# Attention with an MLP on one core: the probability products of two half cycles issued in one block at the end of a cycle

## The chip, the core and the metric

The kernel runs on one core of a Trainium2 chip. The core has five engines that run side by side: TensorE (PE in the profile; its weight loads are PEld) multiplies matrices into PSUM, VectorE (DVE) and ScalarE (ACT) read PSUM and compute elementwise, GpSimd (POOL) works on SBUF only, and SyncE (SP) starts most of the DMA transfers. Each takes its own instructions in order, and semaphores hold one until another engine is done. The metric is the time of one execution in microseconds of the device, less being better.

## The reference: what is computed

One transformer layer on 2048 rows of 512 numbers, with 32 query heads of 16 and one shared key and value head, adaptive layer norms around attention and MLP (`mod` comes from a condition vector).

```python
h = _layernorm(x) * (1 + ca) + sa
q = (h @ wq) -> 32 heads of 16;  k = h @ wk;  v = h @ wv
p = softmax(q k^T * 16 ** -0.5)          # 32 heads x 2048 queries x 2048 keys
x = x + ga * ((p @ v) @ wo)
h = _layernorm(x) * (1 + cb) + sb
x = x + gb * (gelu(h @ w1 + b1) @ w2 + b2)   # 512 -> 1376 -> 512
```

## The kernel before

**Tiles and units.** The queries are cut into 8 blocks of 256 rows and the heads into 8 groups of 4; one pair of the two is a unit, 64 units in all, in order (line 456). A unit goes through the 2048 keys in 8 steps of two 128-key tiles (line 1322). Two steps, X = K and Y = K + 1, make a cycle of the main loop (line 1366), so a unit has four cycles, K = 0, 2, 4, 6, and the loop 256.

**What a step does.** `sexp` (line 584) multiplies a key tile with the queries of two heads, 64 rows of the array by 512 columns, and ScalarE takes the exponential of the product (tile e) into a probability tile p: four such products and exponentials a step, for j = 0, 1 and for s = 0, 1, where s names the upper or lower 64 rows of the array, which work at the same time. The product lands in one PSUM bank of three, e0, e1 or e2, which the caller names; each bank has one buffer (line 591), so the next product in a bank waits until ScalarE has read the one before. `pv` (line 600) multiplies the p tile of a step with the values: 16 products of 128 rows by 32 columns of the array and 256 columns of p, four of them side by side in four column groups, added up over the unit in one PSUM tile (acc, bank v). The p tiles have three buffers (line 590). `end_step` (line 1356) calls `pv` and, after the last step of a unit, `finish_unit`, which has ScalarE copy acc out of PSUM.

**Maxima ahead.** The softmax takes off the row maximum, which is found ahead of time. `Max.step` (line 507) multiplies the queries of a later unit with 512 keys (tile m, three PSUM banks) and VectorE reduces the product to its maximum (line 522). About 8 such steps go into each cycle, four in each half.

**Fill.** The other matrix products (the query projection qps, the output product wops, transposes tp, the MLP's w1ps and w2ps) are cut into batches, and `take` (line 1191) hands one batch to a cycle. Each product of a batch is done in two halves of 64 rows (`half`, line 189): the upper halves in half X of the cycle, the lower ones in half Y, beside the exponent and score products that use the other rows. What follows a batch (bias, GELU, splitting a number into a high and a low part) is put off by `later` and run by `due` at a count of the `clock`, which advances four times a cycle.

**The order of a cycle** (lines 1400 to 1445) is written out by hand, and each engine executes in that order. Half X issues score products, exponent products and the upper halves of the batch; then the products of the step before (`behind`, that is Y of the cycle before); then half Y; then the products of X; Y is left behind for the next cycle. Which bank each exponent product uses is written into three variants:

- heavy, a batch of more than 4.8 (in products of 512 columns; lines 1417 to 1420 and 1433 to 1438): the order of banks is e0, e1, e2, e0 in half X and e0, e1, e2, e0 in half Y, the last of each on the rows of the fill;
- light, a smaller batch (`light_half`, line 1404): each half begins and ends its own rows with e0, and uses e1 and e2 on the other rows;
- without a batch (`plain`, line 1386): e1, e2, e0, e1 in half X and e2, e0, e1, e2 in half Y.

Before the main loop lies a stretch of some 90 us that loads, normalises and projects; after it a tail finishes the last block.

Of the kernel before, what the change touches and what calls it, by code (L numbers as in the profile page):

```python
# [52 lines left out]
def adaln_mqa_mlp(  # L53
# [99 lines left out]
    def due():  # L153
        now = [p for p in pending if p[0] <= clock[0]]
        pending[:] = [p for p in pending if p[0] > clock[0]]
        for _, fn in now:
            fn()
# [31 lines left out]
    def half(one, s):  # L189

        ps, a, b_, first_, last_ = one
        rows = slice(64 * s, 64 * s + 64)
        nc.tensor.matmul(ps, a[rows], b_[rows], start=first_ and s == 0, stop=last_ and s == 1)  # L193
# [390 lines left out]
    def sexp(u, K, j, s, bank):  # L584

        w = blocks[units[u][0]][1]
        qst = qsts[u]
        assert u in placed
        if (u, K) not in ptiles:
            ptiles[u, K] = att.tile([P, 2, 2, 512], F32, name=f"p{u}_{K}", tag="p", bufs=3)  # L590
        e = psum.tile([P, 512], F32, name=f"e{u}_{K}_{j}_{s}", tag="x" if bank == "x" else f"e{bank}", bufs=1)
        rows = slice(64 * s, 64 * s + 64)
        if w == 512:
            kt, rhs = K, qst[rows, j, :]
        else:
            kt, rhs = 2 * K + j, qst[rows].rearrange("p j n -> p (j n)")
        nc.tensor.matmul(e, ks[rows, kt * P:(kt + 1) * P], rhs, start=True, stop=True)  # L597
        nc.scalar.activation(ptiles[u, K][:, j, s, :], e, AF.Exp, scale=0.25)  # L598

    def pv(u, K):  # L600
        w = blocks[units[u][0]][1]
        if K == 0:
            accs[u] = psum.tile([P, w], F32, name=f"acc{u}", tag="v")
        pt = ptiles.pop((u, K))
        for kt in ([K] if w == 512 else [2 * K, 2 * K + 1]):
            for cidx in range(4):
                s, j = divmod(cidx, 2)
                rhs = pt[:, j, s, :] if w == 512 else pt[:, kt - 2 * K, s, j * w:(j + 1) * w]
                ins = nc.tensor.matmul(accs[u][32 * cidx:32 * cidx + 32, :], va[:, kt, :], rhs,  # L609
                                       start=kt == 0, stop=kt == NKT - 1)  # L610
                if kt % 2 or cidx:
                    wait_early(ins)
# [563 lines left out]
    def resume():  # L1176

        go_on(holder[0])

    def advance():  # L1180

        for job in holder or list(queue):
            while not held and job[0] <= clock[0] and go_on(job):
                pass
            if held or holder:
                break

    def put_off(*jobs):
        queue.extend([0, job, False] for job in jobs)

    def take():
        advance()
        return held.pop() if held else None
# [133 lines left out]
    def products(batch):  # L1327

        return sum(b_.shape[-1] * (4 if b_.dtype == F32 else 1) for _, _, b_, _, _ in batch) / 512
# [6 lines left out]
    def issue(*groups):  # L1336

        at = [0.0] * len(groups)
        groups = [list(g) for g in groups]
        while any(groups):  # L1340
            g = min((g for g in range(len(groups)) if groups[g]), key=lambda g: at[g])
            length, fn = groups[g].pop(0)
            fn()
            at[g] += length

    def mixture(a, b):

        out = []
        while a or b:
            if a:  # L1350
                out.append(a.pop(0))
            if b:
                out.append(b.pop(0))
        return out

    def end_step(u, K):

        pv(u, K)
        if K == steps[u] - 1:
            finish_unit(u)  # L1360
            if units[u][1] == NQ - 1:
                put_off(rest(units[u][0], units[u][0] == len(blocks) - 1))

    behind = None
    for u in range(NU):
        for K in range(0, steps[u], 2):
            goal = lead[u] + (lead[u + 1] - lead[u]) * (K + 2) / steps[u]
            goal = min(goal, first[u + QBUFS] if u + QBUFS < NU else first[NU])
            n = max(0, 2 * round((goal - mp.done) / 2))

            def maxes(s, n, first_=1.0, held=None):
                return [(1.0 if i else first_, lambda i=i: mp.step(s, held if i == 2 else None)) if mp.has(s) else (0.0, lambda: None)
                        for i in range(n)]

            def exps(s, which):
                return [(1.0, lambda K=K, j=j, bank=bank: sexp(u, K, j, s, bank)) for K, j, bank in which]

            def halves(batch, s):

                total = products(batch)  # L1380
                if total <= LIGHT:
                    return [(products([one]), lambda one=one: half(one, s)) for one in batch]
                ahead = AHEAD if total > BATCH - 0.5 else (BATCH - (1.5 if batch[-1][4] else 0.5)) / total
                return [(ahead * products([one]), lambda one=one: half(one, s)) for one in batch]

            def plain(s, K, t, n, banks):

                a, b_, c_, d = banks
                ms, other = maxes(s, n), maxes(t, n)

                if not holder and mp.has(s) and n > 1:
                    ms[0] = 1.0, lambda: mp.step(s, tag="x", bufs=1)
                one = mixture(exps(s, [(K, 0, a), (K, 1, c_)]), ms)
                issue(one, exps(t, [(K, 0, b_)]) + other + exps(t, [(K, 1, d)]))

            X, Y = K, K + 1

            due()  # L1400
            batch = take() if behind else None
            light = batch and products(batch) <= LIGHT

            def light_half(s, K):

                mine, fill = exps(s, [(K, 0, 0), (K, 1, 0)]), halves(batch, s) + ([(0.0, go_on_)] if s else [])
                ms, es = maxes(1 - s, n // 2), exps(1 - s, [(K, 0, 1), (K, 1, 2)])
                issue(mine[:1] + fill + mine[1:], ms[:1] + es[:1] + ms[1:3] + es[1:] + ms[3:])

            def go_on_():  # L1410
                resume()
                for fn in reduces or ():
                    fn()

            if light:
                light_half(0, X)
            elif batch:
                groups = [mixture(maxes(1, n // 2, 0.0), exps(1, [(X, 0, 0), (X, 1, 1), (Y, 0, 2)])),
                          halves(batch, 0) + exps(0, [(X, 0, 0)])]
                issue(*(reversed(groups) if batch[0][3] else groups))  # L1420
            else:
                plain(1, X, 0, (n + 2) // 4, (1, 2, 0, 1))
            clock[0] += 1
            due()
            if behind:
                end_step(*behind)
            clock[0] += 1
            due()
            if light:
                reduces = None  # L1430
                light_half(1, Y)
                advance()
            elif batch:

                reduces = [] if batch[-1][4] else None
                issue(mixture(maxes(0, n // 2, 0.0, reduces), exps(0, [(X, 1, 0), (Y, 0, 1), (Y, 1, 2)])),
                      halves(batch, 1) + [(0.0, go_on_)] + exps(1, [(Y, 1, 0)]))
                advance()
            else:
                plain(1, Y, 0, n // 4, (2, 0, 1, 2))  # L1440
            clock[0] += 1
            due()
            end_step(u, X)
            behind = (u, Y)
            clock[0] += 1
            if state["mods"] and "w2" not in preps:
                preps["w2"] = prep_w2()
            if clock[0] >= prepared[0] + PREP and weights and weights[0] in preps:
                prepared[0] = clock[0]
                if next(preps[weights[0]], 0) == 0:  # L1450
                    weights.pop(0)
# [51 lines left out]
```

## Time and profile before

| | |
|---|---|
| median of 3 runs | 1586.05 us (1585.31 to 1586.48) |
| profiled execution | 1589.15 us, its span 1587.3 us |
| TensorE busy in the span | 1562.7 us (98%) |
| VectorE busy | 1406.0 us (89%) |
| ScalarE busy | 1204.3 us (76%) |
| GpSimd busy | 692.8 us (44%) |
| mean granted TensorE clock | 0.992 |

A group's row gives the line, the engine, the operation, output and inputs by the program's names, the count, the busy time and the mean of one, and the idle time ahead of it. In the timeline a row gives the start within the span, the length, and how many equal instructions in a row are merged in it (x16); cuts of the timeline merge differently. A wait "A x <- B y: total, times, longest" says that engine A sat idle ahead of x until B had done y. The ends of matmuls are modelled; their starts are records. In the 1465 us from 80 to 1545 us, in which the main loop lies, the granted TensorE clock was 1.00.

### The profile page before, as it was taken

The numbers are of one execution on the slowest core, as the hardware profiler recorded it, in microseconds if no ns is written. First come the engines' busy times: TensorE is split into PE (matmuls) and PEld (weight loads), VectorE is DVE, ScalarE is ACT, GpSimd is POOL, SyncE is SP. The second block draws the span as 40 slices with busy tenths as digits, with TensorE's granted clock in tenths as the row PEclk, the third lists the DMA queues.
The fourth block names the chain that finished last, engine by engine and source line by source line (L and its number), as shares of the span: only waits on it lengthen the run. The fifth ranks groups of instructions, "written<-read, shape, count | busy, mean of one in ns | idle before, by whom it ended". The sixth has DMA issues, their size and how long they took to land.

```text
span 1587.3 us, 43409 instructions
## 1 busy us (share of the span) xinstructions
PE 1562.7 (98%) x17491; PEld 1043.9 (66%) x17491; DVE 1406.0 (89%) x2491; ACT 1204.3 (76%) x2417; POOL 692.8 (44%) x1242
## 2 busy tenths in 40 slices
PE   5999999999999999999999999999999999999999
PEld 3556655567766676666766676666766677676667
DVE  6889999899999998999999999999999999999715
ACT  5477777778877887778877887778877788778853
POOL 4345447446513472345622464334712465324721
PEclk8899999999999999999999999999999999999999
DMA  7135423312012120212112130212112130121231
GB/s 263 67 108 177 141 70 101 100 33 97 32 56 67 56 86 23 90 35 94 46 40 86 44 99 19 70 54 86 56 32 92 35 108 22 60 72 50 94 139 68
DMA packets 81022, 121.74 MB, mean 77 GB/s; under 512 B 15966, under 2 KB 55646, under 8 KB 80564
## 3 DMA queue, kind: packets, MB, share of 16 engines
q1 hardware_dynamic: 80804, 118.95, 22.6%
q8 instruction: 137, 2.24, 0.6%
q14 instruction: 65, 0.53, 0.1%
q10 hardware_dynamic: 16, 0.00, 0.0%
HBM read 91.13 MB, written 27.27 MB: 75 GB/s over the span
## 4 chain that ended last, share of the span: by engine, by line
PE 94%; ACT 3%; DVE 1%; DMA 1%; issue 0%; SPq 0%; POOL 0%; DVEq 0%; ACTq 0%
PE acc L609 32%; PE e L597 19%; PE m L517 19%; PE w1ps L193 8%; PE w2ps L193 6%; PE wops L193 3%; PE qps L193 2%; ACT p L598 2%; PE w2ps L187 2%; PE w1ps L187 1%; DVE mx L522 1%; PE tp L193 1%; PE kps L164 1%; PE tp L371 0%; PE modr L289 0%; DMA wm<-in_w_mod_dram 0%
## 5 line engine op out<-in xcount | busy, mean ns | idle before, releaser
L522 DVE TENSOR_REDUCE mx<-m 128x1 f32<-128x512 f32 x2048 | 1271.6, 681 | 105.6 <-PE m L517 95.6
L598 ACT ACTIVATE p<-e 128x512 f32<-128x512 f32 x2048 | 1066.6, 601 | 290.5 <-PE e L597 198.9
L517 PE MATMUL m<-ks,qst 64*128 64x512 f32 x2048 | 829.4, 433 | 6.4 <-DVE ve L205 4.9
L597 PE MATMUL e<-qst,ks 64*128 64x512 f32 x2048 | 729.5, 411 | 2.0 <-ACT wqH L334 1.3
L609 PE MATMUL acc<-p,va 128*32 128x256 f32 x8192 | 550.2, 385 | 1.7 <-DMA qst<-dq 1.7
L517 PEld LDWEIGHTS m<-ks,qst 64*128 64x128 f32 x2048 | 367.4, 184 | 104.6 <-DVE mx L522 85.7
L597 PEld LDWEIGHTS e<-qst,ks 64*128 64x128 f32 x2048 | 356.9, 184 | 112.6 <-ACT p L598 102.6
L609 PEld LDWEIGHTS acc<-p,va 128*32 128x32 f32 x8192 | 214.6, 109 | 219.6 <-issue 113.3
L193 PE MATMUL w1ps<-h2H,w1t 64*128 64x256 f32 x1232 | 236.6, 288 | 0.0
L193 PEld LDWEIGHTS w1ps<-h2H,w1t 64*128 64x128 f32 x1232 | 184.0, 185 | 31.7 <-issue 22.2
L566 POOL TENSOR_SCALAR mt<-turned 8x32 f32<-8x32 f32 x256 | 53.5, 209 | 342.7 <-DVE turned L572 330.6
L193 PE MATMUL w1ps<-h2L,w1t 64*128 64x256 f32 x616 | 169.5, 275 | 0.0
L193 PE MATMUL w2ps<-w2H,gH 64*128 64x256 f32 (+1 forms) x546 | 161.0, 295 | 0.0
L193 PE MATMUL w2ps<-w2H,gL 64*128 64x256 f32 (+1 forms) x546 | 153.9, 282 | 0.0
L193 PE MATMUL w2ps<-w2L,gH 64*128 64x256 f32 (+1 forms) x546 | 153.4, 281 | 0.0
L193 PEld LDWEIGHTS w1ps<-h2L,w1t 64*128 64x128 f32 x616 | 113.7, 185 | 0.0
L193 PEld LDWEIGHTS w2ps<-w2H,gH 64*128 64x128 f32 x546 | 100.5, 184 | 11.7 <-issue 5.4
L193 PEld LDWEIGHTS w2ps<-w2H,gL 64*128 64x128 f32 x546 | 100.7, 184 | 1.7
L193 PEld LDWEIGHTS w2ps<-w2L,gH 64*128 64x128 f32 x546 | 100.7, 184 | 1.3
L949 POOL TENSOR_SCALAR tt<-tt 128x256 f32<-128x256 f32 x77 | 31.2, 406 | 143.8 <-ACT tt L948 143.8
L193 PE MATMUL wops<-woH,onH 64*128 64x256 f32 x224 | 67.9, 303 | 0.0
L193 PE MATMUL wops<-woL,onH 64*128 64x256 f32 x224 | 62.2, 278 | 0.0
(220 smaller groups left out, 1613.1 us busy)
## 6 DMA issues: line engine op xcount, KB each, us to landing
w1t<-dw SPq DMA_DIRECT2D x82, 512.0 KB
qst<-dq SPq DMA_DIRECT2D x128, 64.0 KB
do<-oc SPq DMA_DIRECT2D x64, 128.0 KB
dw<-w1s SPq DMA_DIRECT2D x11, 512.0 KB
xt<-in_A_x_dram SPq DMA_DIRECT2D x4, 1024.0 KB
dq<-qH SPq DMA_DIRECT2D x16, 256.0 KB
dq<-qL SPq DMA_DIRECT2D x16, 256.0 KB
qst<-dq SPq DMA_DIRECT2D x128, 32.0 KB
```

What stands on the lines that cost most here:

```text
L164: nc.tensor.matmul(ps, a, b_, start=begin and n == 0, stop=end and n == last)
L187: nc.tensor.matmul(ps, a, b_, start=first_, stop=last_)
L193: nc.tensor.matmul(ps, a[rows], b_[rows], start=first_ and s == 0, stop=last_ and s == 1)
L517: nc.tensor.matmul(m, qsts[u][rows, j, t * P:(t + 1) * P], ks[rows, kc * 512:(kc + 1) * 512], start=True, stop=True)
L522: nc.vector.tensor_reduce(out=self.mx[u][:, i, kc:kc + 1], in_=m, axis=AX.X, op=ALU.max)
L566: nc.gpsimd.tensor_scalar(out=mt[:, g:g + 32], in0=turned[g:g + 4 * T, :], scalar1=1.0, scalar2=0.0, op0=ALU.mult, op1=ALU.add)
L597: nc.tensor.matmul(e, ks[rows, kt * P:(kt + 1) * P], rhs, start=True, stop=True)
L598: nc.scalar.activation(ptiles[u, K][:, j, s, :], e, AF.Exp, scale=0.25)
L609: ins = nc.tensor.matmul(accs[u][32 * cidx:32 * cidx + 32, :], va[:, kt, :], rhs, start=kt == 0, stop=kt == NKT - 1)
L949: nc.gpsimd.tensor_scalar(out=tt, in0=tt, scalar1=1.0, scalar2=1.0, op0=ALU.mult, op1=ALU.add)
```

## The change

The products of the step before are issued in the middle of the cycle only in the first cycle of a unit (K = 0), where they are the last ones of the unit before and its sums are then copied out. In the other three cycles they are issued at the end of the cycle, directly ahead of the products of X: 32 products in one block where there were two blocks of 16 with half Y between them. The first line only keeps the condition for taking a batch as it was, as `behind` may now be empty. Banks, buffers, batches and the counts of the clock are untouched.

```diff
@@ -1398,7 +1398,7 @@
             due()
-            batch = take() if behind else None
+            batch = take() if u or K else None
             light = batch and products(batch) <= LIGHT
@@ -1422,8 +1422,9 @@
                 plain(1, X, 0, (n + 2) // 4, (1, 2, 0, 1))
             clock[0] += 1
             due()
-            if behind:
+            if behind and K == 0:
                 end_step(*behind)
+                behind = None
             clock[0] += 1
             due()
             if light:
@@ -1440,6 +1441,8 @@
                 plain(1, Y, 0, n // 4, (2, 0, 1, 2))
             clock[0] += 1
             due()
+            if behind:
+                end_step(*behind)
             end_step(u, X)
             behind = (u, Y)
             clock[0] += 1
```

## The prediction

> **What bounds the kernel now.** I read the page first, for the shares and the chain of waits.
>
> ```profile
> PE 1562.7 (98%) x17491; PEld 1043.9 (66%) x17491; DVE 1406.0 (89%) x2491; ACT 1204.3 (76%) x2417; POOL 692.8 (44%) x1242
> ...
> PE 94%; ACT 3%; DVE 1%; DMA 1%; issue 0%; SPq 0%; POOL 0%; DVEq 0%; ACTq 0%
> PE acc L609 32%; PE e L597 19%; PE m L517 19%; PE w1ps L193 8%; PE w2ps L193 6%; PE wops L193 3%; PE qps L193 2%; ACT p L598 2%; PE w2ps L187 2%; PE w1ps L187 1%; DVE mx L522 1%; PE tp L193 1%; PE kps L164 1%; PE tp L371 0%; PE modr L289 0%; DMA wm<-in_w_mod_dram 0%
> ```
>
> TensorE ends the run, and the probability products (acc, line 609) are the largest piece of the chain. The reader is to see that 98% is not 98% of useful streaming: an end of a matmul is modelled, so time between two kinds of work can hide in it. Next come the waits, which say who could be late once TensorE is faster.
>
> ```profile
> ACT p L598 <- PE e L597: 198.9, 336, 0.9
> ...
> PEld e L597 <- ACT p L598: 102.6, 290, 0.6
> DVE mx L522 <- PE m L517: 95.6, 255, 3.2
> ```
>
> ScalarE and VectorE wait for TensorE more than it waits for them. The third view is the timeline of TensorE through one cycle of the main loop, a cycle of the first MLP product, K greater than 0.
>
> ```profile
> 394.36 1.07 PE L609 MATMUL acc<-p,va 128*32 128x256 f32 x16
> 395.03 0.40 PE L609 MATMUL acc<-p,va 128*32 128x256 f32 x4
> 395.36 0.38 PE L193 MATMUL w1ps<-h2H,w1t 64*128 64x256 f32 x1
> 395.37 0.49 PE L517 MATMUL m<-ks,qst 64*128 64x512 f32 x1
> ...
> 395.70 0.39 PE L597 MATMUL e<-qst,ks 64*128 64x512 f32 x1
> ...
> 396.40 0.39 PE L517 MATMUL m<-ks,qst 64*128 64x512 f32 x1
> ...
> 396.63 0.39 PE L597 MATMUL e<-qst,ks 64*128 64x512 f32 x1
> ...
> 396.85 0.42 PE L597 MATMUL e<-qst,ks 64*128 64x512 f32 x1
> 396.87 0.41 PE L517 MATMUL m<-ks,qst 64*128 64x512 f32 x1
> 397.21 1.07 PE L609 MATMUL acc<-p,va 128*32 128x256 f32 x16
> 398.21 0.50 PE L517 MATMUL m<-ks,qst 64*128 64x512 f32 x1
> ...
> 400.07 1.07 PE L609 MATMUL acc<-p,va 128*32 128x256 f32 x16
> ```
>
> The cycle is 400.07 - 394.36 = 5.71 us: block of 16 probability products, half X (395.36 to 396.87), block, half Y (398.21 to 399.76), block. The fourth view is ScalarE's timeline over the same stretch, the one on which everything below turns.
>
> ```profile
> 396.13 2.08 ACT L598 ACTIVATE p<-e 128x512 f32<-128x512 f32 x4 [0.51 <-PE e L597]
> ```
>
> TensorE is through with half X at about 397.2, but ScalarE finishes its four exponentials only at 396.13 + 2.08 = 398.21. That is the instant at which half Y starts today. The middle block is what TensorE does in the meantime.
>
> **What the edit removes.** In 3 cycles of 4, so 64 units x 3 = 192 cycles, the middle block goes to the end and stands directly before the other one. No instruction is added or dropped. One pass between two kinds of products disappears. From the rows: last round of a block at 395.03, next product 395.36, 0.33; last product of a half 396.87, next block 397.21, 0.34; first pair of products after a block 395.37 to 395.70, 0.33. Inside a half, two products of the same half of the array are 396.63 - 396.40 = 0.23 apart, and the two halves of the array take turns, so one starts each 0.12. Inside a block one round of four costs less than the 0.33: this cut of a block shows two rounds.
>
> ```profile
> 397.45 0.61 PE L609 MATMUL acc<-p,va 128*32 128x256 f32 x8
> ```
>
> Two rounds take 0.61, one took 0.40, so a round is 0.21; three rounds from 394.36 to 395.03 give 0.22. I take 0.215. The pass costs 0.33 - 0.22 = 0.11 behind the block, 0.34 - 0.12 = 0.22 ahead of it and 0.10 in the first pair: 0.43. The Trainium skill's page "TensorEngine Tiling (Array Packing)", Key Properties, has a rule for it: a change of tiling mode drains the TensorE; the blocks are 128*32 and the halves 64*128, and the gaps agree. By that rule alone the edit is a gain, the first rival below.
>
> **What the edit uncovers: heavy cycles.** Line 1419 ends half X with an exponent product in bank e0, and the first exponent product of half Y (line 1436, `(X, 1, 0)`) is in e0 again. That bank has one buffer, so this product waits for the exponential of the fourth product of half X, the end of ScalarE's run above, 398.21. Queued behind it on TensorE, in program order, are the whole fill of half Y, three exponent products, three score products for VectorE and both blocks. How fast TensorE goes on after such a wait shows in a half that has one already, in a cycle without a fill:
>
> ```profile
> 475.61 0.50 PE L597 MATMUL e<-qst,ks 64*128 64x512 f32 x1
> 476.03 1.07 PE L609 MATMUL acc<-p,va 128*32 128x256 f32 x16
> ...
> 478.21 0.50 PE L597 MATMUL e<-qst,ks 64*128 64x512 f32 x1
> ```
>
> ```profile
> 474.95 2.06 ACT L598 ACTIVATE p<-e 128x512 f32<-128x512 f32 x4 [0.50 <-PE e L597]
> ```
>
> The product of 475.61, half X's last, uses the bank of the first (order 1, 2, 0, 1 below). Four exponentials in 2.06 at 0.60 each (mean of line 598 below) stand (2.06 - 0.60) / 3 = 0.49 apart; the first ends at 475.55, and TensorE goes on 0.06 later, with the block behind it waiting too.
>
> ```profile
> L598 ACT ACTIVATE p<-e 128x512 f32<-128x512 f32 x2048 | 1066.6, 601 | 290.5 <-PE e L597 198.9 <-PE m L517 67.1 <-PE qps L193 21.4
> ```
>
> So half Y restarts at 398.21 + 0.06 = 398.27, 0.06 later than it starts today, though nothing lies in front of it. Only its first score product is done by then; the fill of 12 and the exponent product at its end, which set its length, are not, so I give it today's length. Then come four more rounds, 4 x 0.215 = 0.86. A heavy cycle grows by 0.06 + 0.86 = 0.92: the saved 0.43 and the covered time are both lost in the wait. No row shows a block directly behind a block. Its bounds are 0.84 by the smaller round (4 x 0.21) and 1.00 by the chain, which puts 1.00 on each block; the round is nearest.
>
> ```profile
> 397.28 1.00 PE acc L609 x16
> ```
>
> **Light cycles.** With a fill of at most 4.8 (`light_half`), half X ends on e0 and half Y begins with it.
>
> ```profile
> 440.74 0.50 PE L597 MATMUL e<-qst,ks 64*128 64x512 f32 x1
> ```
>
> ```profile
> 438.53 2.07 ACT L598 ACTIVATE p<-e 128x512 f32<-128x512 f32 x4 [0.67 <-PE e L597]
> ```
>
> Restart at 438.53 + 2.07 + 0.06 = 440.66 in place of 440.74: -0.08 + 0.86 = +0.78. Light cycles with only five small products issue their e0 product third, and half Y began at 449.05:
>
> ```profile
> 446.74 1.78 ACT L598 ACTIVATE p<-e 128x512 f32<-128x512 f32 x3 [0.66 <-PE m L517]
> ```
>
> ```profile
> 449.05 0.49 PE L597 MATMUL e<-qst,ks 64*128 64x512 f32 x1
> ```
>
> 446.74 + 1.78 + 0.06 = 448.58: -0.47 + 0.86 = +0.39.
>
> **Cycles without a fill** turn through the banks (1, 2, 0, 1, then 2, 0, 1, 2). The last product of half Y needs the fifth exponential, which ScalarE, going on without a pause, starts at 474.95 + 4 x 0.49 = 476.91 and ends at 477.51. So that product is at 477.57 and not 478.21: -0.64 + 0.86 = +0.22.
>
> **Edits that cost nothing.** The probability tiles (three buffers) that a cycle writes held the two steps whose products now end the cycle before, ahead of its first exponent product. Transfers and the steps put off keep their place: the counter still advances four times a cycle. The DMA waits attached to probability products move at most one half later, and the product that needs the data carries its own wait.
>
> **The sum.** Counting the fills between blocks in the timeline, the 192 changed cycles are 124 heavy, 41 light, 13 with five small products, 14 without a fill: 124 x 0.92 + 41 x 0.78 + 13 x 0.39 + 14 x 0.22 = 114 + 32 + 5 + 3 = 154 us. The profiled execution took 1589.15 us (span 1587.3), so 1743; it is 3.1 above the median of the runs, 1586.05, on which it is 1740.
>
> **Rivals.** *Faster.* The wait stays covered and only the passes count: 192 x 0.43 = 83, so 1503. It decides if ScalarE's fourth exponential is done when TensorE reaches half Y, about 397.1. Against it: 398.21 in the row, more than 1 us late, in a stretch without anything else on ScalarE. Chance 0.05; it needs the two e0 tiles not to collide, against lines 1419 and 1436.
>
> *VectorE takes over.* With no wait on ScalarE, eight score products come in one stretch through three banks.
>
> ```profile
> 395.31 3.07 DVE L522 TENSOR_REDUCE mx<-m 128x1 f32<-128x512 f32 x5
> 398.74 0.69 DVE L522 TENSOR_REDUCE mx<-m 128x1 f32<-128x512 f32 x1 [0.36 <-PE m L517]
> ```
>
> A reduction alone takes 0.69, in a run one each (3.07 - 0.69) / 4 = 0.60, the first 0.54 after its product (the second of the five, 395.91, against 395.37). The eighth product needs the fifth reduction's end: 0.54 + 4 x 0.60 + 0.69 + 0.06 = 3.69; then about 0.38 to the blocks, and 0.67 + 0.86 + 0.33 to the next half: 5.93, or +0.22, so 192 x 0.22 = 42 and 1628. For it: VectorE is 89% busy. Against: ScalarE's wait ends later. Chance 0.04.
>
> *The wait is there, but half Y packs closer behind it:* it is one product of 0.23 shorter on one half of the array and has no slow first pair, 0.10. Then heavy cycles grow by 0.59, and 1740 - 124 x 0.33 = 1699. For it: the score product is indeed done. Against: the fill sits on the other half. Chance 0.10.
>
> **How the numbers follow.** The forecast, 1740, has 0.81. The range reaches from a little under the closer packing, 1695, to 1770: the block at 1.00 adds 192 x 0.14 = 27. Within 0.2% (3 us, about what a measurement of this kernel can tell) lies no case; I leave 0.01 between the gain and the losses. Faster 0.05, slower 0.94.
>
> **What would show it.** Right: on the page PE's share falls and ScalarE's line 598 enters the chain; in the waits "PEld e <- ACT p" grows from 102.6 by about 150 us or more; in a heavy cycle half Y's first exponent product starts 0.06 after the fourth exponential, and two blocks take 32 products with no gap; cycles with K = 0 stay at their length. Wrong: half Y starting within 0.3 of half X's last product, or changed cycles under 5.7 us, or new idle time ahead of the score products that ends with VectorE.

## The result, and the profile after

The changed kernel takes 1736.4 us (median of 4 runs, 1734.46 to 1737.54) against 1586.26 us of the kernel before in the same comparison (1585.31 to 1589.97): the ratio is 1.094, with a 95% interval of 1.092 to 1.0961. It is slower by 150 us. The profiled execution took 1736.75 us, its span 1735.0.

The page of the changed kernel, engines and chain:

```profile
PE 1602.1 (92%) x17491; PEld 1075.8 (62%) x17491; DVE 1411.4 (81%) x2491; ACT 1212.1 (70%) x2417; POOL 692.1 (40%) x1242
...
PE 72%; ACT 22%; DVE 3%; DMA 2%; issue 1%; SPq 0%; POOL 0%; ACTq 0%; DVEq 0%; POOLq 0%
PE acc L609 28%; ACT p L598 21%; PE e L597 17%; PE m L517 10%; PE w1ps L193 5%; PE w2ps L193 4%; DVE mx L522 2%; PE wops L193 2%; PE w2ps L187 1%; PE qps L193 1%; PE w1ps L187 1%; DMA xt<-in_A_x_dram 1%; PE kps L164 1%; DMA qst<-dq 1%; PE tp L193 0%
```

The instructions are the same in number. The exponentials of line 598 went from 2% to 21% of the chain: ScalarE now holds TensorE up, though ScalarE itself is busy for 70% of the span and not 76%. The waits of the changed kernel say where (engine and line, whom it waited for, total, times, longest):

```profile
PEld e L597 <- ACT p L598: 223.5, 370, 1.3
...
PE e L597 <- ACT p L598: 106.4, 178, 1.0
...
PEld m L517 <- DVE mx L522: 68.3, 202, 1.1
```

The weight loads of the exponent products waited 102.6 us for an exponential before and wait 223.5 us now. The products' own wait, 106.4 us, has no row in the list before. It is not to be added to the 223.5, as it is the same stretch seen a second time: in the cycle below, the weight load (idle for 0.83) and the product (idle for 0.52) both start at 643.71. Here is this one heavy cycle with K > 0 in TensorE's timeline, cut down to the places that matter, and under it ScalarE's:

```profile
639.84 1.05 PE L609 MATMUL acc<-p,va 128*32 128x256 f32 x16
...
642.31 0.42 PE L597 MATMUL e<-qst,ks 64*128 64x512 f32 x1
642.32 0.87 PE L517 MATMUL m<-ks,qst 64*128 64x512 f32 x2
643.71 0.50 PE L597 MATMUL e<-qst,ks 64*128 64x512 f32 x1 [0.52 <-ACT p L598]
643.71 0.50 PE L193 MATMUL w1ps<-h2H,w1t 64*128 64x256 f32 x2
...
645.52 1.93 PE L609 MATMUL acc<-p,va 128*32 128x256 f32 x32
647.38 0.38 PE L193 MATMUL w2ps<-w2H,gH 64*128 64x256 f32 x1
```

```profile
641.58 2.08 ACT L598 ACTIVATE p<-e 128x512 f32<-128x512 f32 x4 [1.46 <-PE e L597]
```

Half X's last exponent product starts at 642.31, the next one only at 643.71, 0.05 after ScalarE's run of four ends (641.58 + 2.08 = 643.66), and the fill of half Y starts with it. In between lie only two score products (merged in the row of 642.32), of which the second already belongs to half Y. The 32 products then take 647.38 - 645.52 = 1.86, where one block takes 1.00 (397.21 to 398.21 before): the second block costs 0.86, and the pass between it and the half is indeed saved. It is saved in front of a wait.

Cycle lengths, from the first product of a cycle to the first of the next, averaged over the cycles of a kind in the two traces (K > 0, with score products):

| kind of cycle | number | before | after | change | predicted |
|---|---|---|---|---|---|
| heavy | 121 | 5.74 | 6.59 | +0.85 | +0.92 |
| light | 41 | 5.55 | 6.29 | +0.75 | +0.78 |
| five small products | 10 | 5.69 | 6.38 | +0.69 | +0.39 |
| no fill (one outlier, 7.72 after, left out) | 13 | 5.28 | 5.60 | +0.32 | +0.22 |
| K = 0, unchanged order | 63 | 5.71 | 5.69 | -0.02 | 0 |

121 x 0.85 + 41 x 0.75 + 10 x 0.69 + 13 x 0.32 = 145 us. The seven changed cycles left are that outlier and six at the end of the loop, where no score products remain (the prediction had counted those six among the heavy ones and the ones with five small products); they add 9 us. With the cycles of K = 0 the loop grew by 152 us between the two traces; the stretch ahead of it happened to be 4 us shorter in the trace after.

The cycle shown is typical. Over the 121 heavy cycles, on average, half Y's fill starts 2.91 us after the cycle's first product before and 2.90 after; from there to the block at the cycle's end it is 1.83 in both; the block itself takes 1.00 before and 1.86 after.

### The profile page after: what moved, and what is told of

Read it like the earlier page. It is cut to its first block, busy times and chain, and to the rows that moved or that the text cites. A ratio compares the mean times of both kernels' runs of the same rounds, so it can differ in the third digit from the quotient of the medians.

```text
span 1735.0 us, 43409 instructions
## 1 busy us (share of the span) xinstructions
PE 1602.1 (92%) x17491; PEld 1075.8 (62%) x17491; DVE 1411.4 (81%) x2491; ACT 1212.1 (70%) x2417; POOL 692.1 (40%) x1242
## 4 chain that ended last, share of the span: by engine, by line
PE 72%; ACT 22%; DVE 3%; DMA 2%; issue 1%; SPq 0%; POOL 0%; ACTq 0%; DVEq 0%; POOLq 0%
PE acc L609 28%; ACT p L598 21%; PE e L597 17%; PE m L517 10%; PE w1ps L193 5%; PE w2ps L193 4%; DVE mx L522 2%; PE wops L193 2%; PE w2ps L187 1%; PE qps L193 1%; PE w1ps L187 1%; DMA xt<-in_A_x_dram 1%; PE kps L164 1%; DMA qst<-dq 1%; PE tp L193 0%
## 5 line engine op out<-in xcount | busy, mean ns | idle before, releaser
L597 PE MATMUL e<-qst,ks 64*128 64x512 f32 x2048 | 761.9, 418 | 108.5 <-ACT p L598 106.4
L597 PEld LDWEIGHTS e<-qst,ks 64*128 64x128 f32 x2048 | 358.4, 184 | 254.4 <-ACT p L598 223.5
L609 PE MATMUL acc<-p,va 128*32 128x256 f32 x8192 | 513.2, 385 | 0.9 <-DMA qst<-dq 0.8
L517 PEld LDWEIGHTS m<-ks,qst 64*128 64x128 f32 x2048 | 369.6, 184 | 94.5 <-DVE mx L522 68.3
L609 PEld LDWEIGHTS acc<-p,va 128*32 128x32 f32 x8192 | 235.1, 110 | 206.1 <-issue 68.6
```

The source lines that it names most:

```text
L517: nc.tensor.matmul(m, qsts[u][rows, j, t * P:(t + 1) * P], ks[rows, kc * 512:(kc + 1) * 512], start=True, stop=True)
```

## The experiments

The theory: in the kernel before, the middle block costs nothing, as TensorE would otherwise wait for the exponential that frees bank e0; put at the end it costs its full length. The rivals: TensorE's own work and its passes set the time; the block of 32 is slow in itself or starves VectorE.

**Leave the middle block out** of the kernel before.

```diff
-            if behind:
+            if behind and K == 0:
                 end_step(*behind)
```

> The kernel before, without the middle block where K > 0: the probability products of the steps 1, 3 and 5 of each unit are left out, and 3072 of the 8192 are gone (sums are kept above 1e-30 ahead of their reciprocals, a few small VectorE operations). Theory, the middle block only fills the wait for ScalarE's fourth exponential in bank e0: half Y starts when it did, so a heavy cycle changes by about +0.06, a light one by -0.08, one with five small products by -0.47, one without a fill by up to -0.64; sum 124 x 0.06 - 41 x 0.08 - 13 x 0.47 - 14 x 0.64 = -11, so about 1575 us. Rival, TensorE's own work sets the time and the blocks are on its path: each of the 192 blocks takes its 0.86 and its pass of 0.43 with it, 248 us, so about 1338 us.

Measured: 1579.65 us, ratio 0.9951 (0.9932 to 0.9971). More than a third of the probability products are gone, and the time falls by 0.5%. A heavy cycle of this kernel, TensorE and then ScalarE:

```profile
390.02 1.07 PE L609 MATMUL acc<-p,va 128*32 128x256 f32 x16
...
392.51 0.42 PE L597 MATMUL e<-qst,ks 64*128 64x512 f32 x1
392.53 0.87 PE L517 MATMUL m<-ks,qst 64*128 64x512 f32 x2
393.93 0.49 PE L597 MATMUL e<-qst,ks 64*128 64x512 f32 x1 [0.53 <-ACT p L598]
...
395.77 1.07 PE L609 MATMUL acc<-p,va 128*32 128x256 f32 x16
```

```profile
391.80 2.08 ACT L598 ACTIVATE p<-e 128x512 f32<-128x512 f32 x4 [0.61 <-PE e L597]
```

Between 392.51 and 393.93 lie two score products and then nothing but the wait, which ends 0.05 after 391.80 + 2.08, and the cycle is still 395.77 - 390.02 = 5.75 long. So are the heavy cycles on average, 5.74 before and 5.75 here. The expected 1575 is missed by 5 us, the rival's 1338 by 240 us.

**Issue the middle block as well**, in the kernel after: the same products once in the middle and once more at the end.

```diff
             if behind and K == 0:
                 end_step(*behind)
                 behind = None
+            elif behind:
+                pv(*behind)
```

> The kernel after, with the middle block issued as well: the products of the steps 1, 3 and 5 of each unit are added twice, once in the middle and once at the end, so 3072 products and 192 passes more than in the kernel after. Theory of the wait: TensorE stands idle there for at least as long as a block takes, so the added work is nearly free, between 1730 and 1755 us. Rival, TensorE is the bound: 192 x (0.86 + 0.43) = 248 us more, about 1984 us.

Measured: 1743.52 us, ratio 1.0981 (1.0961 to 1.1001), 7 us above the kernel after for 3072 products more, and within the range expected. Heavy cycles are at 6.59, as in the kernel after. The two runs together: in heavy cycles the block in the middle is free, present or not, in either kernel. In the other cycles it is not quite free. Left out of the kernel before, it shortens light cycles by 0.08, those with five small products by 0.18 and those without a fill by 0.41 (5.28 to 4.88); issued in the kernel after, it lengthens them by 0.07, 0.18 and 0.48. That makes about 10 us in either run, the size of the 8 and 7 us by which the two times moved.

**Half of it.** One key tile of the step before stays in the middle.

```diff
+            elif behind:
+                pv(*behind, parts=(0,))
...
             if behind:
-                end_step(*behind)
+                pv(*behind, parts=(1,))
             end_step(u, X)
```

> The kernel after, but of the step before, the first key tile's 8 products stay in the middle of the cycle and only the second key tile's 8 go to the end. Theory of the wait: 8 products and their passes end before ScalarE's fourth exponential, so half Y starts with the wait as in the kernel after, and only 8 products (0.43) come on top at the end: of the 151 us by cycles that the kernel after lost, about half stays, 60 to 85 us, so about 1650 to 1670 us. Rival, a block of 32 is slow in itself or starves VectorE: 24 products are still long, and the loss is over 110 us, above 1696. Rival, passes set the time: two blocks a cycle are back and the time is that of before, 1586.

Measured: 1652.01 us, ratio 1.0407 (1.0386 to 1.0427): 65 us of the 150. Heavy cycles rose by 0.42 (5.74 to 6.16), the 8 products at the end, 2 x 0.215, and light ones by 0.31. Half Y's fill starts 2.90 after the cycle's first product, as in the kernels before and after. The loss goes with what is put at the end. That passes set the time is refuted: this kernel has as many as the kernel before.

**Earlier exponential.** In the kernel after, half X issues its second e0 product ahead of the one in e2.

```diff
-                groups = [mixture(maxes(1, n // 2, 0.0), exps(1, [(X, 0, 0), (X, 1, 1), (Y, 0, 2)])),
+                ms, es = maxes(1, n // 2, 0.0), exps(1, [(X, 0, 0), (X, 1, 1), (Y, 0, 2)])
+                groups = [mixture(ms, es[:2]) + es[2:],
```

> The kernel after, with the order of the last two exponent products of half X exchanged in cycles with a fill: the second product in e0 is issued ahead of the one in e2, so its exponential is ScalarE's third and not its fourth. No work is added or dropped. Theory of the wait: half Y restarts one exponential earlier, at most 0.49 and in heavy cycles about 0.33 (the product is issued 1.49 after the half's start, its exponential takes 0.43 to begin and 0.60): 124 x 0.33 + 41 x 0.4 = 57 us less, so about 1680 us, between 1670 and 1700. Rival, VectorE or the length of the block sets the time: no change, 1736.

Measured: 1715.88 us, ratio 1.0802 (1.0779 to 1.0825). The gain is 20 us, not 57, and the time lies outside the expected 1670 to 1700. In the trace heavy cycles with K > 0 went from 6.59 to 6.33, near what was expected, but light ones stayed (6.29 to 6.31): in them the exchange moved half X's last exponent product itself back, to 1.65 us after the cycle's first product from 1.18 to 1.40. And the cycles with K = 0, which the exchange changed too and the expectation had left out, grew from 5.69 to 5.83. So the exchange was made again in the heavy cycles with K > 0 alone:

> The kernel after, with the second e0 product of half X issued ahead of the one in e2, now only in heavy cycles with K > 0. Theory of the wait: those 124 cycles lose the 0.21 to 0.28 that they lost in the exchange made everywhere (54 x 0.28 + 31 x 0.26 + 21 x 0.21 + 18 x 0.26 = 32 us), and the cycles that it made longer are as in the kernel after: 1704 us, between 1698 and 1712. Rival, the gain of the exchange came from elsewhere: about 1716 again.

Measured: 1703.45 us, ratio 1.0744 (1.0728 to 1.076), as expected. Heavy cycles are at 6.34. TensorE and ScalarE in one of them:

```profile
581.87 0.50 PE L597 MATMUL e<-qst,ks 64*128 64x512 f32 x1 [0.23 <-ACT p L598]
...
583.67 1.93 PE L609 MATMUL acc<-p,va 128*32 128x256 f32 x32
```

```profile
580.03 2.27 ACT L598 ACTIVATE p<-e 128x512 f32<-128x512 f32 x4 [1.49 <-PE e L597]
```

The exponent product and the fill of half Y now begin at 581.87, while the run of four lasts until 582.30: they no longer wait for the fourth, but for the third, which ends at 581.81. The block of 32 is still behind them and still takes 1.86, so it is the wait that got shorter. The same exchange in the kernel before:

> The kernel before, with the same exchange in heavy cycles with K > 0. Theory of the wait: in the kernel before, half Y starts when the middle block ends, and its first e0 product comes 0.34 later, so an exponential that is ready earlier buys nothing: 1586 us, within 0.3%. Rival, the kernel before is held by ScalarE as well: up to 32 us less, 1554.

Measured: 1595.11 us, ratio 1.0057 (1.004 to 1.0074): a little slower, so the expected "no change" is missed by 0.3%, and the rival's gain is refuted. Heavy cycles went from 5.74 to 5.82. The trace shows why, in averages counted from the cycle's first product: half X's last exponent product starts at 1.64 and not at 1.51, the middle block follows at 1.96 and not at 1.86, and half Y's fill starts when that block is through, now 0.37 after the exponential. So with the exponential out of the way, the block is what half Y waits for. In the kernel before the two end together (the block at 2.86, the exponential at 2.85), which is why the block is free there and an earlier exponential gains nothing. No kernel here that issues all the products beats the kernel before.

**Slower ScalarE.** Two small copies ahead of the third exponential, in heavy cycles with K > 0, in both kernels.

```diff
+                es = exps(1, [(X, 0, 0), (X, 1, 1), (Y, 0, 2)])
+                if K:
+                    es[2] = (1.0, lambda third=es[2][1]: (nc.scalar.copy(spare, ident[:, :64]), nc.scalar.copy(spare, ident[:, :64]), third()))
```

> The kernel after, with two extra copies of 128x64 on ScalarE ahead of the third exponential of half X in heavy cycles with K > 0 (a copy of that size took 0.212 us, two in a row 0.2 to 0.42). Theory of the wait: half Y restarts later by all of it: 124 x 0.2 to 0.42 = 25 to 52 us more, 1761 to 1788. Rival, VectorE or the block sets the time: 1736.

Measured: 1790.07 us, ratio 1.129 (1.1273 to 1.1307), 54 us above the kernel after and 2 us above the expected range; heavy cycles 6.59 to 6.99, +0.39.

> The kernel before with the same two copies. Theory of the wait: the e0 product of half Y has 0.28 to spare (ready 0.06 after the exponential, issued 0.34 after it), so what is over that comes through: 124 x 0 to 0.14 = 0 to 17 us more, 1586 to 1603, and in any case less than in the kernel after. Rival, the kernel before waits for ScalarE all the same: as much as in the kernel after.

Measured: 1635.52 us, ratio 1.032 (1.0302 to 1.0337), 50 us above the kernel before; heavy cycles 5.74 to 6.12, +0.38. Here the theory's number failed and the rival's came in: heavy cycles of the kernel before have no slack at all. The timeline with the copies (lines are one further down), TensorE and then ScalarE:

```profile
391.28 1.07 PE L610 MATMUL acc<-p,va 128*32 128x256 f32 x16
392.28 0.50 PE L518 MATMUL m<-ks,qst 64*128 64x512 f32 x1
392.73 0.49 PE L598 MATMUL e<-qst,ks 64*128 64x512 f32 x1
392.73 0.50 PE L194 MATMUL w1ps<-h2H,w1t 64*128 64x256 f32 x2
```

```profile
391.17 0.52 ACT L1421 COPY spare<-ident 128x64 f32<-128x64 f32 x2
391.59 1.08 ACT L599 ACTIVATE p<-e 128x512 f32<-128x512 f32 x2
```

The score product starts when the block is through, at 392.28. The exponent product waits for ScalarE (391.59 + 1.08 = 392.67), and the fill, on the other half of the array and in a bank of its own, starts with it at 392.73 and not before. The fill is behind the exponent product in program order, and the wait holds both. In the kernel before, without the copies, the two rows are:

```profile
398.27 0.50 PE L193 MATMUL w1ps<-h2H,w1t 64*128 64x256 f32 x2
398.55 0.39 PE L597 MATMUL e<-qst,ks 64*128 64x512 f32 x1
```

The expectation had looked at the exponent product's start (398.55), which has 0.28 to spare, and not at the fill's (398.27), 0.06 after the exponential's end (398.21), which sets the length of half Y. That holds throughout: in all 121 heavy cycles the fill starts 0.05 to 0.09 after the fourth exponential before, and 0.06 after it with the copies.

**VectorE's part** in the cycles with five small products: its two operations on finished maxima, half a cycle later.

```diff
-            later((0 - clock[0]) % 4 + 1, reduce)
+            later((0 - clock[0]) % 4 + 3, reduce)
```

> The kernel after, with VectorE's two small operations on a finished unit's maxima (lines 571 and 572) put off by half a cycle, to the end of half Y. Theory: in the cycles with five small products and K = 2, half Y's last score product waits for a PSUM bank that VectorE frees late because these two operations (0.17 and 0.21) stand ahead of its reduction; with them gone the cycle falls from 6.38 to about 6.1 to 6.2 us, towards the +0.39 of the prediction, and heavy cycles keep 6.57 to 6.64. Rival, the extra 0.3 of these cycles comes from ScalarE or the block: they stay at 6.38. The whole changes by some 3 us at most.

Measured once: 1730.01 us; that is too little to call a change of the whole. But these ten cycles went from 6.38 to 6.08, 0.39 above the 5.69 of before, while heavy cycles kept their 6.59. In the kernel after, TensorE and VectorE in such a cycle:

```profile
688.43 0.50 PE L517 MATMUL m<-ks,qst 64*128 64x512 f32 x1
688.86 1.93 PE L609 MATMUL acc<-p,va 128*32 128x256 f32 x32
```

```profile
687.32 0.18 DVE L571 TENSOR_REDUCE mm<-mx 128x8 f32<-128x32 f32 x1
687.60 0.21 DVE L572 STREAM_TRANSPOSE turned<-mm 128x32 f32<-128x32 f32 x1
687.73 1.84 DVE L522 TENSOR_REDUCE mx<-m 128x1 f32<-128x512 f32 x3
```

The first of the three reductions merged in the last row ends at 688.38, and the score product of 688.43, ahead of the block, takes its bank.

Other banks for half Y, so that it need not wait for half X, were not tried. As the program is written, the turn of e0 is also what keeps the second half of a fill behind the first, and both add up in one PSUM bank; no run shows what would happen without it.

## Why the prediction was right

**The place of the loss** was right: the wait for bank e0 takes the place of the middle block. The profile after shows it (0.05 after the exponential, 0.06 predicted), and the first two experiments show it from both sides, in heavy cycles.

**The second block** at the end was right: 0.86 predicted, 0.86 in the timeline, and half of it costs half.

**Heavy cycles** were put at +0.92 and measure +0.85. The mis-sized term is the restart, "0.06 later than it starts today". Today's half Y was counted from its score product; its fill, which sets its length, already starts 0.06 after the exponential, in the row 398.27. So half Y restarts no later than before (2.91 and 2.90 us into the cycle), and only the 0.86 remains. The run of the kernel before with a slower ScalarE shows that there was nothing to spare.

**Light cycles** were right within 0.03 on average.

**Five small products** (+0.39 predicted, +0.69 measured) failed on VectorE: the step that took the restart as the only thing that moves left out that a half Y that starts 0.47 earlier also asks VectorE for a bank 0.47 earlier. With VectorE's two operations moved away, the predicted 0.39 is there. **Cycles without a fill** (+0.22 and +0.32) show the same in the trace, a score product that starts just after a reduction ends; that was only read there. Both are small terms, 23 cycles together.

**The sum**, 154 us predicted and 150 measured, is closer than its parts, and that is in part luck. By the traces, all heavy cycles together brought 105 us and not 114, light ones 31 and not 32, and the two small kinds 18 and not 8; the errors cancel.

**The signs** that were named came in but for two. The wait "PEld e <- ACT p" grew by 121 us and not by 150 or more. And cycles without a fill are under 5.7 us after the change (5.60), which was named as a sign of being wrong, although the predicted +0.22 puts them there as well. The chances given to the slower cases add up to 0.95, where 0.94 is stated.

The rivals fell as follows. The faster one fell because the exponential is about 1 us late when TensorE is through with half X (last exponent product at 642.31, exponential's end 643.66). VectorE's fell by the heavy cycles, which follow ScalarE's end in the kernel after wherever it was moved, and by the wait of the score products' weight loads for VectorE, which went down from 85.7 to 68.3 us. The closer packing fell because the fill, not the score product, sets half Y's length: 1.83 us from the fill's start to the block, before and after.

The saved passes, 0.43 each by the rows of the prediction, show in no cycle length, since they are saved in front of a wait. What a pass is worth where nothing waits, no run here shows.

## What to carry to other kernels

Work that stands between a product and the next use of its PSUM bank may be cover and not load: compare its length with the time that the bank's reader needs, and leave it out once as a test before you move it. It is free only up to the length of the wait: with the exponential moved ahead in the kernel before, the block was the limit. Look for the instruction that stands first in program order behind a wait and at everything queued behind it, on all parts of the array, and not at the waiting instruction alone.

## What the runs showed of the hardware

Two parts of TensorE's array that work on their own data did not pass each other at a wait: in the kernel before with the slower ScalarE, the fill on 64 rows started with the waiting exponent product on the other 64, both at 392.73, though by the program the fill neither uses that exponential's result nor writes its bank. Once the wait is over, starts do cross: in the kernel before, the first fill product of half Y starts at 398.27 and the exponent product that is issued ahead of it at 398.55.
